# Moving the forward D2 reshuffles and the lower filter halves to ScalarE's DMA queue, with table maskings as broadcast VectorE products

## Chip, cores, metric

One core of one Trainium2 chip. The time is device microseconds (us) of one execution. A lower time is better. The profile is of one execution of each kernel.

## What is computed

The kernel computes the forward pass and all gradients of a block with two parts. The first part is a spectral filter on the layer-normalised input (2048 x 448). The second is an MLP over the 2048 tokens.

```python
def _A_ref(x, w_r, w_i):                       # spectral filter
    X = rfft2(x.astype(float32), axes=(-2, -1))
    return irfft2(X * (w_r + 1j * w_i), s=(S, D)).astype(bfloat16)
def _B_ref(x, w1, b1, w2, b2):                 # MLP over tokens, F = 1792
    u = gelu(einsum("bsd,sf->bdf", layernorm(x), w1) + b1)
    return transpose(einsum("bdf,fs->bds", u, w2) + b2)
h  = x + _A_ref(layernorm(x), A_w_r, A_w_i)
h2 = h + _B_ref(layernorm(h), B_w1, B_b1, B_w2, B_b2)
# outputs: h2 and the gradients for x, w_r, w_i, w1, b1, w2, b2 from grad_out
```

Only the forward transform of the filter, some 20 to 70 us into the kernel, is touched here. It has two stages. In the first, TensorE makes rows of the half-transformed input. ScalarE and VectorE evacuate them (copy them out) from PSUM, where TensorE writes its results, into staging tiles, and eight DMAs (the reshuffles, u = 0 to 7) scatter the staging tiles over the partitions of `D2`. The second stage multiplies with tables `Ut` and `Vt` and needs all of `D2`. Between these matmuls TensorE does others of the MLP's backward part (`ps_mm` in the profile), whose transposed blocks of `B_w2` are loaded by DMAs, the transpositions.

## The kernel before, where it is touched

SyncE issues every DMA here, in program order. `nc.sync` is SyncE, `nc.scalar` and `sc` are ScalarE, `ve` is VectorE, `gp_` is GpSimd.

```python
# the tables: eight masked products of 256 elements each, on whichever engine has room
for j in range(4):
    m = msk[:, j:j + 1]
    dj = d1[:, :, :, j - 1] if j else dst[:, :, 112:128]
    for o, c in ((d0[:, :, :, j], 0), (dj, 1)):
        if load[1] + 0.24 < load[0] + 0.38:
            ve.tensor_scalar(out=o, in0=cv[:, :, :, c], scalar1=m, scalar2=None, op0=ALU.mult)
        else:
            sc.activation(out=o, in_=cv[:, :, :, c], func=ACT.Copy, scale=m)
        yield
...
def w_load():      # spectral filter: four DMAs for the real part, then four for the imaginary part
    for c_, d in ((0, A_w_r), (1, A_w_i)):
        for p0, p1, j0, j1, row, dims in (...):
            nc.sync.dma_start(out=W_rows[p0:p1, c_, j0:j1, :], in_=bass.AP(...))
            yield
...
def row_b(h, quarters=False):
    ...            # one row: matmuls, then the evacuation into cs
    if c:
        defer(RESH_LAG, lambda: nc.sync.dma_start(out=D2[u:u + 121:8]..., in_=cs...), cs)   # reshuffle u
...
def load_w2T():    # one transposed block of B_w2 into a ring of five buffers
    nc.sync.dma_start_transpose(out=wT, in_=B_w2[j * P:(j + 1) * P, :]...)
...
def fwd_x(c2):     # begins the second stage
    if c2 == 0:
        for kind in "TWWWWTTT":        # T: a held transposition; W: an imaginary filter load
            if kind == "W":
                next(w_loads)
            elif held_w2:
                held_w2.pop(0)()
```

Program order on SyncE is therefore: reshuffles with real filter loads and transpositions between them, then reshuffle 7, then one held transposition, four imaginary filter loads, and more held transpositions. Nothing written in the program says that the later ones must follow reshuffle 7. They follow it only because SyncE waits for that reshuffle's evacuation. (In the profile, `ps_ff` and `ps_mm` are PSUM tiles, L218 and L82 are the helpers through which matmuls and the work of ScalarE and VectorE pass, and `rS`, `r`, `rX`, `UTt` are what an evacuation writes; `r<-r` is a reshuffle.)

## Time and profile before

| | before |
|---|---|
| time, median of 3 (range) | 359.86 us (359.79 to 361.12) |
| span, granted clock of the profiled run | 358.5 us, 0.989 |
| TensorE busy | 341.3 us, 95% |
| TensorE waits in 20 to 70 us | A 1.6 (ScalarE evacuation), B 1.4 (transposed block of B_w2), C 1.0 (ScalarE evacuation), 0.5 (VectorE) |
| last reshuffle: issued, landed | 46.66, 49.8 us |
| first matmul of the second stage | 50.34 us |

The lines of the profile stand in the prediction. "Landed" here and below is the time of the last semaphore count of a DMA in the trace. The granted clock is the share of full speed that TensorE was allowed.

### The profile page before, as it was taken

The numbers are of one execution on the slowest core, as the hardware profiler recorded it, in microseconds if no ns is written. First come the engines' busy times: TensorE is split into PE (matmuls) and PEld (weight loads), VectorE is DVE, ScalarE is ACT, GpSimd is POOL, SyncE is SP. The second block draws the span as 40 slices with busy tenths as digits, with TensorE's granted clock in tenths as the row PEclk, the third lists the DMA queues.
The fourth block names the chain that finished last, engine by engine and source line by source line (L and its number), as shares of the span: only waits on it lengthen the run. The fifth ranks groups of instructions, "written<-read, shape, count | busy, mean of one in ns | idle before, by whom it ended". The sixth has DMA issues, their size and how long they took to land.

```text
span 358.5 us, 6455 instructions
## 1 busy us (share of the span) xinstructions
PE 341.3 (95%) x2133; PEld 183.5 (51%) x2133; DVE 252.4 (70%) x676; ACT 214.9 (60%) x460; POOL 64.0 (18%) x227
## 2 busy tenths in 40 slices
PE   5888998899999999999999999999999999999994
PEld 2455665555645555555555555544445444455551
DVE  5896626991884888685327888784497766489895
ACT  4659836965986555503221455565478776478883
POOL 8667000000220000001001111110000000045462
PEclk9699999999999999999999999999999999999999
DMA  8999989747999999997976999969975878999995
GB/s 207 292 208 241 192 184 160 167 140 267 279 289 352 301 349 228 236 248 211 218 180 131 194 205 205 214 178 266 282 198 187 239 204 227 252 183 230 249 305 212
DMA packets 147673, 81.63 MB, mean 228 GB/s; under 512 B 95480, under 2 KB 139768, under 8 KB 147384
## 3 DMA queue, kind: packets, MB, share of 16 engines
q1 hardware_dynamic: 147640, 81.23, 94.1%
q8 instruction: 16, 0.26, 0.3%
q14 instruction: 17, 0.14, 0.1%
HBM read 27.56 MB, written 23.89 MB: 144 GB/s over the span
## 4 chain that ended last, share of the span: by engine, by line
PE 76%; DVE 8%; ACT 7%; DMA 4%; issue 3%; SPq 1%; POOL 0%; ACTq 0%; DVEq 0%
PE ps_mm L218 63%; PE ps_ff L218 13%; DVE r L82 4%; DMA rO<-in_B_w_dram 2%; ACT rO L82 2%; DVE stats L82 2%; DMA rA<-in_A_x_dram 1%; ACT rG L82 1%; ACT Ut L82 1%; DVE rA L82 1%; DVE rS L82 1%; SPq L297 1%; ACT r L82 1%; ACT Vt L82 1%; ACT rX L82 0%
## 5 line engine op out<-in xcount | busy, mean ns | idle before, releaser
L218 PEld LDWEIGHTS <-r 128*128 128x128 bf16 (+2 forms) x660 | 61.7, 104 | 50.8 <-issue 3.8
L218 PEld LDWEIGHTS <-rS 128*128 128x128 bf16 (+2 forms) x496 | 40.3, 98 | 39.3 <-issue 7.6
L218 PE MATMUL ps_mm<-rD,r 128*128 128x448 bf16 x224 | 44.5, 352 | 0.0
L82 ACT CAST rO<-ps_mm 128x512 bf16<-128x512 f32 (+1 forms) x63 | 33.7, 576 | 12.5 <-PE ps_mm L218 12.1
L218 PE MATMUL ps_mm<-rC,rE 128*128 128x448 bf16 x144 | 36.1, 370 | 3.2 <-DMA rC<-in_grad_out_dram 3.2
L218 PEld LDWEIGHTS <-rst 128*128 128x128 bf16 (+1 forms) x320 | 23.9, 97 | 29.3 <-issue 13.8
L82 ACT CAST r<-ps_ff 128x452 bf16<-128x452 f32 x58 | 33.5, 577 | 8.6 <-PE ps_ff L218 8.2
L218 PE MATMUL ps_mm<-r,rst 128*128 128x512 bf16 (+3 forms) x192 | 36.6, 353 | 0.0
L218 PE MATMUL ps_mm<-rB,r 128*128 128x448 bf16 x160 | 31.2, 352 | 0.1
L218 PE MATMUL ps_mm<-rG,rst 128*128 128x512 bf16 (+1 forms) x128 | 28.2, 380 | 0.0
L82 ACT ACTIVATE r<-ps_mm,rstd_h 128x448 bf16<-128x448 f32 x16 | 10.2, 635 | 26.0 <-PE ps_mm L218 26.0
L82 ACT ACTIVATE r<-rC 128x448 bf16<-128x448 bf16 x16 | 9.1, 572 | 26.8 <-DMA out_dram<-r 13.2
L82 DVE SCALAR_TENSOR_TENSOR r<-ps_mm,b2col,r 128x448 bf16<-128x448 f32 x16 | 10.9, 683 | 19.9 <-PE ps_mm L218 18.2
L82 DVE CAST rO<-ps_mm 128x512 bf16<-128x512 f32 x17 | 11.6, 689 | 16.3 <-PE ps_mm L218 15.4
L82 ACT ACTIVATE rG<-rG 128x896 bf16<-128x896 bf16 x14 | 13.3, 952 | 14.9 <-DVE rG L82 14.7
L218 PEld LDWEIGHTS <-rO 128*128 128x128 bf16 (+1 forms) x165 | 15.6, 98 | 12.1 <-DMA rO<-in_B_w_dram 1.7
L218 PE MATMUL ps_mm<-rE,rS 128*128 128x448 bf16 x112 | 21.5, 352 | 0.0
L82 ACT CAST rG<-ps_mm 128x512 bf16<-128x512 f32 (+1 forms) x35 | 17.2, 540 | 6.9 <-PE ps_mm L218 6.7
L218 PE MATMUL ps_mm<-rC,rO 128*128 128x448 bf16 x80 | 19.1, 352 | 1.4 <-DMA rO<-in_B_w_dram 1.4
L1180 POOL TENSOR_SCALAR lcol<-lcol 128x1 f32<-128x1 f32 x16 | 8.5, 532 | 65.1 <-ACT r L82 65.1
L218 PEld LDWEIGHTS <-rE 128*128 128x128 bf16 x148 | 14.3, 100 | 11.2 <-issue 4.9
L218 PE MATMUL ps_ff<-csI,rAT 113*128 113x224 bf16 (+1 forms) x108 | 19.0, 298 | 0.4 <-ACT rAT L82 0.2
(198 smaller groups left out, 645.4 us busy)
## 6 DMA issues: line engine op xcount, KB each, us to landing
out_dram<-rO SPq DMA_DIRECT2D x34, 256.0 KB
r<-in_B_w_dram SPq DMA_DIRECT2D x5, 1024.0 KB
r<-r SPq DMA_DIRECT2D x16, 226.0 KB
r<-r SPq DMA_DIRECT2D x32, 113.0 KB
rS<-in_B_w_dram SPq DMA_DIRECT2D x4, 896.0 KB
out_dram<-rG SPq DMA_DIRECT2D x10, 256.0 KB
rO<-in_B_w_dram SPq DMA_DIRECT2D x2, 1024.0 KB
out_dram<-rG SPq DMA_DIRECT2D x10, 192.0 KB
```

The costliest lines, as they stand in the source:

```text
L82: fn(**kw)
L218: nc.tensor.matmul(out, lhsT=lhsT, rhs=rhs, start=start, stop=stop)
L297: nc.sync.dma_start_transpose(out=wT, in_=B_w2[j * P:(j + 1) * P, :].rearrange("f (t c) -> f t c", c=P))
L1180: gp_.tensor_scalar(out=m1, in0=ms, scalar1=-1.0 / D, scalar2=None, op0=ALU.mult)
```

## The change

Intent: take ScalarE's small maskings away, give the freed time to DMA issue, and free SyncE so that held transpositions and filter loads go out earlier. The diff, cut to its core:

```diff
+    mskb = mem.tile([P, 1, 1, 4], BF16, name="mskb")
+    gp_.tensor_copy(out=mskb[:, 0, 0, :], in_=msk)
-            for j in range(4):
-                ...                       # eight products of 256 elements, VectorE or ScalarE
+            for out, c, j in ((d0, 0, 0), (d1, 1, 1)):
+                n = 4 - j
+                nc.vector.tensor_tensor(out=out, in0=cv[:, :, :, c:c + 1].broadcast_to([P, 16, 16, n]),
+                                        in1=mskb[:, 0:1, 0:1, j:4].broadcast_to([P, 16, 16, n]), op=ALU.mult)
+                yield True
+            evac_mask(dst[:, :, 112:128], cv[:, :, :, 1], msk[:, 0:1])
...
-                nc.sync.dma_start(out=W_rows[p0:p1, c_, j0:j1, :],
+                resh_eng(p0 == 0).dma_start(out=W_rows[p0:p1, c_, j0:j1, :],
...
-    def resh_eng():
-        _ei[0] += 1
-        return nc.sync
+    def resh_eng(on_act=True):
+        if not on_act:
+            return nc.sync
+        load[0] += 0.55
+        return nc.scalar
...
-            defer(RESH_LAG, lambda: nc.sync.dma_start(out=D2[u:u + 121:8]...
+            defer(RESH_LAG, lambda: resh_eng(not quarters).dma_start(out=D2[u:u + 121:8]...
```

`load` is the program's own estimate of each engine's work, by which it hands out evacuations while it is built. Each DMA issued on ScalarE adds 0.55 us to it, so the change can also move evacuations from ScalarE to VectorE.

More of the change, by code (lines that the diff above doesn't have):

```diff
@@ L463, with evac_mask @@
     comp_ring = ring(rO, 0, 2, 512)
+    mskb = mem.tile([P, 1, 1, 4], BF16, name="mskb")
+    def evac_mask(out, in_, m):
+        if load[1] + 0.43 < load[0] + 0.7:
+            ve.tensor_scalar(out=out, in0=in_, scalar1=m, scalar2=None, op0=ALU.mult)
+        else:
+            load[0] += 0.3
+            sc.activation(out=out, in_=in_, func=ACT.Copy, scale=m)
     def gen_UV():
@@ L502, in gen_UV @@
             d1 = dst[:, :, 64:112].rearrange("p g (l f) -> p g l f", f=3)
-            for j in range(4):
-                m = msk[:, j:j + 1]
-                dj = d1[:, :, :, j - 1] if j else dst[:, :, 112:128]
-                for o, c in ((d0[:, :, :, j], 0), (dj, 1)):
-                    if load[1] + 0.24 < load[0] + 0.38:
-                        ve.tensor_scalar(out=o, in0=cv[:, :, :, c], scalar1=m, scalar2=None, op0=ALU.mult)
-                    else:
-                        sc.activation(out=o, in_=cv[:, :, :, c], func=ACT.Copy, scale=m)
-                    yield
+            for out, c, j in ((d0, 0, 0), (d1, 1, 1)):
+                n = 4 - j
+                load[1] += 0.06 + 256.0 * n / 960.0
+                nc.vector.tensor_tensor(out=out, in0=cv[:, :, :, c:c + 1].broadcast_to([P, 16, 16, n]),
+                                        in1=mskb[:, 0:1, 0:1, j:4].broadcast_to([P, 16, 16, n]), op=ALU.mult)
+                yield True
+            evac_mask(dst[:, :, 112:128], cv[:, :, :, 1], msk[:, 0:1])
+            yield
     Rp = rO[:, 1536:1536 + P]
@@ L692, in row_b @@
         if c:
-            defer(RESH_LAG, lambda: nc.sync.dma_start(out=D2[u:u + 121:8].rearrange("p g c k -> p (g c k)"),
+            defer(RESH_LAG, lambda: resh_eng(not quarters).dma_start(out=D2[u:u + 121:8].rearrange("p g c k -> p (g c k)"),
                                                       in_=cs.rearrange("p x c k -> p (x c k)")), cs)
```

## The prediction

> **What bounds the kernel now.** I read the page's busy shares first, then the table of stretches, then the waits of TensorE, then the chain that ended last between 20 and 70 us, and last the timelines of the single engines and of the SyncE queue. The busy shares:
>
> ```profile
> PE 341.3 (95%) x2133; PEld 183.5 (51%) x2133; DVE 252.4 (70%) x676; ACT 214.9 (60%) x460; POOL 64.0 (18%) x227
> ```
>
> TensorE is the bound: 358.5 - 341.3 = 17.2 us of the span are all that it is not busy, and a change that leaves its work alone can win only from these. The change touches the forward transform, which by the tiles' use lies between 20 and 70 us:
>
> ```profile
> 20.00:30.00 10.00, 7.90 (x59) 4.77 (x57) 9.96 (x37) 7.40 (x15) 7.66 (x30) 1.00 1.00 208
> 30.00:40.00 10.00, 9.94 (x84) 7.04 (x85) 6.43 (x23) 8.67 (x18) 4.57 (x21) 1.00 1.13 244
> 40.00:50.00 10.00, 9.95 (x73) 6.24 (x71) 4.55 (x11) 5.20 (x11) 0.11 (x1) 1.00 0.79 144
> 50.00:60.00 10.00, 9.13 (x72) 5.87 (x70) 5.99 (x18) 6.97 (x18) 0.11 (x1) 1.00 1.18 191
> 60.00:70.00 10.00, 8.48 (x54) 5.27 (x55) 7.96 (x18) 8.28 (x13) 0.00 (x0) 1.00 0.95 197
> ```
>
> The columns are the stretch, its length, then busy time of PE, PEld, DVE, ACT, POOL, the clock, the DMA share and GB/s. TensorE is idle 10 - 7.90 = 2.1, then 0.06, 0.05, 0.87 and 1.52 us: 4.6 us together, 1.3% of the span. That is the ceiling of the whole change. The waits of TensorE in this window name nearly all of it:
>
> ```profile
> PE ps_ff L218 <- ACT rS L82: 1.6, 1, 1.6
> PE ps_mm L218 <- DMA rO<-in_B_w_dram: 1.4, 1, 1.4
> PE ps_ff L218 <- ACT rX L82: 1.0, 1, 1.0
> PE ps_ff L218 <- DVE rX L82: 0.5, 1, 0.5
> ```
>
> Call the first wait A, the second B, the third C. The chain shows what stands ahead of A: two and three table maskings on ScalarE round one row's evacuations, and only then the evacuation that TensorE waits for at 30.07 us.
>
> ```profile
> 25.79 1.08 ACT Ut L82 x2
> 26.87 0.47 ACT rS L82
> 27.34 0.44 ACT r L82
> 27.77 1.81 ACT Ut L82 x3
> 29.59 0.43 ACT rS L82
> ```
>
> B is a late transposed block of B_w2. SyncE's timeline shows why it is late:
>
> ```profile
> 46.66 0.53 SPq L693 DMA_DIRECT2D r<-r  x1
> 47.28 2.26 SPq L297 DMA_TRANSPOSE rO<-in_B_w_dram  x1
> 49.59 2.35 SPq L583 DMA_DIRECT2D rB<-in_A_w_i_dram  x4
> 52.05 4.87 SPq L297 DMA_TRANSPOSE rO<-in_B_w_dram  x1
> ```
>
> SyncE issues in program order. The last reshuffle of D2 (L693) waits until 46.66 us for its evacuation; the held transposes and the imaginary filter loads (L583) stand behind it. The transpose of 52.05 us is the one that TensorE waits for; the chain gives it 8.48 us to 60.5.
>
> C belongs to another part: from 62.1 to 68.0 us ScalarE copies five filter quarters of 0.95 us each between evacuations. The change doesn't take those copies away.
>
> **What the Trainium skill says.** "VectorE: DVE Perf Modes", What auto-detection actually checks: two elements per cycle need every tensor to be 16-bit with step 1 or -1. The trace agrees for packed operands: the 128x904 bf16 products took 625 ns, the 128x448 ones 384 to 392, so 456 more elements cost about 237 ns, 1.9 per ns at 0.96 GHz. The new products read one operand with an innermost step of zero, so I take one element per cycle; no row of this trace has that form.
>
> "ScalarE: Activation LUTs", What ACT_TABLE_LOAD costs: 186 ns + 0.833 N, some 93 ns more per pointer operand, back-to-back overlap 93 ns. For 256 elements with a pointer scale that is about 0.40 us from one to the next. The trace differs: two maskings took 1.08 us and three 1.81 in the chain, 0.54 to 0.60 each. I use the trace.
>
> "DMA: Bandwidth & Descriptors", Queues, rings and completion order and Issuing engines are not separate DMA queues: SP and ACT each own one ring per DMA engine, each ring is consumed in order, the rings are served in turn, and a second issuer saves sequencer time but no bandwidth. The trace agrees on the order within a ring: the reshuffle issued at 36.62 us, behind a filter load, has its last semaphore count at 44.6, 8.0 us later, while that of 46.66, with little ahead of it, is complete at 49.8, 3.1 us later.
>
> **The change part by part.**
>
> 1. Table maskings. Removed: 16 products of 256 elements. On ScalarE ran 6 of Ut and 5 of Vt, at 0.55 us each 11 x 0.55 = 6.0 us; on VectorE 2 and 3, at about 0.33 us back to back (three in 0.99) 5 x 0.33 = 1.7 us. Added: per table one product of 1024 and one of 768 elements on VectorE, at 0.96 per ns plus 0.06 us back to back (0.625 - 904/1920 = 0.15 of fixed time, less 0.09 that neighbours overlap): 1.13 + 0.86 = 2.0 us, so 4.0 us for both; and one remaining masking per table, 0.33 or 0.55 us on either engine. GpSimd gets one four-element copy. ScalarE loses about 5 to 6 us, VectorE gains 2.3 to 3.0.
>  On the path: A. Of the Ut maskings five stand in ScalarE's row between 25.79 and 29.59 us, about 2.8 us, and the sixth follows. Without them the evacuation at 29.59 can come as soon as its matmuls end, near 28 us. VectorE is full until 30 us (9.96 of 10), and the Ut products put 2.0 - 0.7 = 1.3 us more there. It is not late then, though: its row scalings were 0.5 us ahead of the matmuls that read them near 23.8 us and 1.7 us ahead near 27.5, and after 33.3 us VectorE idles 2.6 us. I count A down from 1.6 to about 0.4 us: -1.2 us.
>
> 2. D2 reshuffles. Eight issues of 0.53 to 0.68 us leave SyncE for ScalarE's sequencer: 8 x 0.55 = 4.4 us, two of them before 31 us, six between 33 and 47. Two filter loads of 450 KB follow, 1.2 us. So ScalarE gives back almost all that part 1 freed, 5.6 against 5 to 6 us, but spread over 25 us in which it has room (8.67 of 10 between 30 and 40, 5.20 between 40 and 50). An evacuation there is needed only a row later, some 1.75 us, so one issue of 0.55 us in front of it costs TensorE little. I count +0.2.
>
> 3. Freed SyncE. Its next transpose then waits only for its ring slot, whose matmuls end near 34 us, not for the reshuffle at 46.66. I expect it at about 36 us instead of 47.3, the upper imaginary loads near 38 to 40, and the transpose that B waits for near 40 us, when its own slot is read out (38.9 us). It is then down long before 59 us, and B vanishes: -1.4 us. ScalarE and VectorE sat idle waiting for matmuls through most of B (1.55 and 1.84 us), so I expect their work behind it to shift along, and C to stay at about 1.0.
>
> 4. What the earlier transfers collide with. By the packets in the trace, a transpose is 2048 packets of 256 bytes of some 19 ns, /16 engines = 2.4 us; the upper imaginary loads also about 2.4. Between 35 and 48 us the queue now carries about 11 us of work in 13 us; two transposes and these loads add 7.2, so the engines are full until about 49. The last reshuffle competes with them. The second-stage matmul at 50.3 us needs all eight reshuffles; the last one's data landed at 49.8, so only 0.5 us is spare, and if A is gone that matmul is due at 49.1. ScalarE's own ring gives the reshuffle a share in turn, 128 packets of 1808 bytes, so I expect a wait of 0 to 1.5 us: +0.7.
>
> Sum: -1.2 + 0.2 - 1.4 + 0.7 = -1.7 us, and 359.86 - 1.7 = 358.2. After 105 us TensorE is 10.00 of 10 in every stretch to 150, so a shift earned before it is carried through. A few tenths more may come from the earlier start of later D3 reshuffles and of the filter placing on SyncE: I predict 357.9 us.
>
> **The rivals.** (i) The reshuffles land late. If ring turns favour the long filter packets (some 550 ns against 140), the last reshuffle could be 3 to 5 us late, and the second stage starts late: 360 to 363 us. For it speaks the DMA share above 1.1 around it; against it, that few such packets are left by 46 us and that the loads' lower halves are in the same ring as the reshuffles, behind them. (ii) VectorE becomes the bound of the first rows: it is full from 10 to 30 us, and if the broadcast products cost 1.5 us instead of 1.13, the row scalings come late and A is replaced by a wait of like size: 359 to 360. Against it speaks its idle time after 33 us. (iii) Everything works: A, B and the 0.5 us wait go, and the evacuations are shared out so that C shrinks too: 4.6 us at most minus small rests, 355.5 to 356.5. (iv) B's gain is taken by ScalarE, which is 8.28 of 10 from 60 to 70 us; then C grows by some 1 us: about 359.
>
> **Range and chances.** The middle, between (i) and (iii), is 357.9; eight times in ten 355.9 to 360.8. Over 2% faster would be under 352.7, 7.2 us of gain against a ceiling of 4.6: 0.02. Over 2% slower, above 367.1, needs seven late us at the second stage: 0.03. Within 2%: 0.95.
>
> **What would show it.** Right: no TensorE wait on the ScalarE rS evacuation above 0.6 us between 25 and 31; no wait on a transposed block near 59; SyncE's first held transpose before 40 us; broadcast products of 1.2 and 0.95 us as the trace counts them; second-stage matmuls starting within 1 us of 50. Wrong: a wait of the second stage on D2 over 2 us, row matmuls waiting for VectorE's rX or rS over 1 us in all after 23 us, or C above 2 us.

## The result, and the profile after

| | before, same rounds | after |
|---|---|---|
| median (range), 4 runs each | 359.83 us (359.02 to 361.12) | 369.56 us (368.17 to 369.9) |
| ratio, 95% interval | | 1.026 [1.0219, 1.030] |
| span and clock of the profiled run | 358.5 us, 0.989 | 368.1 us, 0.970 |
| first matmul of the second stage | 50.34 us | 61.86 us |

The changed kernel is 2.6% slower. A ratio here is the mean time of one kernel's fast runs over that of the other's of the same rounds, so it is not quite the ratio of the medians.

**Where the time went.** The stretches of the kernel after, with the columns as in the prediction (PE, PEld, DVE, ACT, POOL, clock, DMA share, GB/s):

```profile
30.00:40.00 10.00, 6.53 (x53) 4.20 (x52) 7.18 (x22) 3.88 (x8) 7.15 (x22) 0.94 1.14 227
40.00:50.00 10.00, 7.97 (x38) 4.75 (x37) 1.55 (x3) 3.54 (x8) 0.00 (x0) 0.50 1.07 197
50.00:60.00 10.00, 10.00 (x65) 6.25 (x63) 3.81 (x8) 2.83 (x5) 0.11 (x1) 0.87 1.10 183
```

Compare 30 to 40 us: before, PE was 9.94 busy and ACT 8.67. Now they are 6.53 and 3.88. Both idle. From 40 to 50 us PE looks fairly busy, but the clock column says 0.50: half speed, and 38 matmul instructions are counted where there had been 73. TensorE's waits from 18 to 75 us:

```profile
PE ps_ff L218 <- ACT rS L82: 3.5, 1, 3.5
PE ps_ff L218 <- ACT r L82: 2.0, 1, 2.0
PE ps_ff L218 <- DMA r<-r: 1.6, 1, 1.6
```

(The list goes on with 1.0 us for a transposed block at 28.56 us.) The first two name ScalarE evacuations; the third is the second stage waiting for the last reshuffle. Wait A at 28 to 30 us is gone, but the 1.0 us for the transposed block stand in its place. B at 59 us is gone, and C fell from 1.0 to 0.7. Most of what the prediction wanted to win was won, and more was lost.

**Why ScalarE was late.** Its timeline; the bracket is the idle time before a line and what ended it:

```profile
38.04 0.63 ACTq L592 DMA_DIRECT2D rB<-in_A_w_r_dram  x1
38.71 0.53 ACT L82 CAST rD<-ps_mm 128x448 bf16<-128x448 f32 x1 [5.27 <-DMA rE<-in_B_w_dram]
...
45.40 0.57 ACTq L704 DMA_DIRECT2D r<-r  x1
46.01 0.54 ACT L82 CAST r<-ps_ff 128x452 bf16<-128x452 f32 x1 [5.35 <-DMA rB<-in_A_w_r_dram]
...
56.33 0.54 ACTq L704 DMA_DIRECT2D r<-r  x1
```

Read the second line. An evacuation that reads only PSUM is said to have waited 5.27 us for a transposition of B_w2, with which it shares no data. What waited was the DMA issue in the line above, and the evacuation stood behind it, because ScalarE runs in order. The DMA records in the trace, which carry the number of each DMA's completion semaphore (the counter by which it reports its end), show why the issue waited. The DMAs of SyncE and ScalarE use eight such semaphores in turn, one set for both engines. The instruction records name the waits: the first issue waits for semaphore 107, the second for 101, and each came when the previous user of that semaphore had landed:

| DMA on ScalarE | its semaphore's previous user | previous user landed | issued |
|---|---|---|---|
| real filter load, lower half (L592) | transposition issued on SyncE at 32.26 | 38.02 | 38.04 |
| reshuffle 4 (L704) | real filter load issued on SyncE at 38.57 | 45.30 | 45.40 |

Before, no such wait occurs here: between 20 and 70 us SyncE's waits are for TensorE and for evacuations, and the semaphore of reshuffle 4, which went out at 36.62 us, had been free since 30.98. A rival reading, that ScalarE cannot issue while SyncE issues a transposition, fails in the same trace: reshuffle 5 went out on ScalarE at 48.83 us, inside SyncE's issue of a transposition from 46.80 to 52.96. The Trainium skill, "DMA: Bandwidth & Descriptors", Anatomy of one DMA, says that DMA engines do not wait on semaphores and that such a wait is made on the issuing sequencer. The trace agrees: 5.27 and 5.35 us of ScalarE's idle time.

**Why the clock fell.** TensorE stood idle for 3.5 us up to 39.79 us. The clock record of the trace has half speed from 38.89 to 52.54 us, and in this time the same matmuls took 1.32 us in place of 0.73. Three matmuls of 128x448 before, then after:

```profile
19.84 0.73 PE L218 MATMUL ps_mm<-rC,rE 128*128 128x448 bf16 x3
```

```profile
46.98 1.32 PE L218 MATMUL ps_mm<-rC,rE 128*128 128x448 bf16 x3
```

The Trainium skill, "TensorE: Matmul & The Clock Gate", What's actually happening, says that an idle window of about 3.4 us halves the clock and that about 3.4 us of sustained work restores it. The trace differs in the first: half speed began 2.6 us after TensorE's last matmul had ended at 36.32 us. The same section calls the window free-running, that is, not started by the kernel, and with that the return agrees: half speed lasted 13.65 us, four times the section's 3.41 us. In the first three of these four stretches TensorE still had idle time (the rest of the 3.47 us, then the 2.03 us up to 46.60). The fourth was full, and at its end the clock came back.

**The sum.** The second stage started 61.86 - 50.34 = 11.5 us later. TensorE's idle waits up to there are 0.54 + 1.05 + 3.47 + 2.03 + 1.55 = 8.6 us after, and 0.36 + 0.54 + 1.62 = 2.5 us before: 6.1 us more. At half clock, TensorE was busy some 0.2 + 8.0 + 2.6 = 10.8 us (the 2.6 from the mean clock 0.87 of 50 to 60 us), and half of that, 5.4 us, is lost speed. 6.1 + 5.4 = 11.5, an estimate that fits. B (1.4 us) and 0.3 us of C are then won back, and the span ends 9.6 us later.

**What SyncE did with its freedom.** Its queue after:

```profile
39.69 5.11 SPq L297 DMA_TRANSPOSE rO<-in_B_w_dram  x1
44.84 1.86 SPq L592 DMA_DIRECT2D rB<-in_A_w_i_dram  x3
46.80 6.16 SPq L297 DMA_TRANSPOSE rO<-in_B_w_dram  x1
```

Before, these three came at 47.28, 49.59 and 52.05 us, behind reshuffle 7. Now the first precedes reshuffles 4 to 7 (issued 45.40, 48.83, 54.28, 56.33 us) and all three precede 5 to 7. Before, the block of the first was first read at 53.07 us and that of the last at 60.57: work that is needed later goes ahead of work that is needed at 50. Reshuffle 7 was issued 9.7 us later than before and took 5.4 us instead of 3.1.

One more thing is slow, early on: a transposition issued on SyncE at 19.41 us and reshuffle 0, issued on ScalarE at 19.52, landed at 28.52 and 26.43 us. Before, the transposition of 19.66 landed at 24.4. By the packets in the trace, the DMA engines moved 121 GB/s from 22 to 28 us in the kernel after (112 to 129 in stretches of 2 us), against 197 before.

### The profile page after: what moved, and what is told of

The parts are those of the page before. It is cut to its first block, busy times and chain, and to the rows that moved or that the text cites. A ratio compares the mean times of both kernels' runs of the same rounds, so it can differ in the third digit from the quotient of the medians.

```text
span 368.1 us, 6441 instructions
## 1 busy us (share of the span) xinstructions
PE 346.2 (94%) x2133; PEld 185.4 (50%) x2133; DVE 255.4 (69%) x675; ACT 210.7 (57%) x451; POOL 68.3 (19%) x228
## 4 chain that ended last, share of the span: by engine, by line
PE 76%; DMA 7%; DVE 6%; ACT 6%; issue 2%; SPq 2%; POOL 0%; ACTq 0%; DVEq 0%
PE ps_mm L218 62%; PE ps_ff L218 14%; DVE r L82 3%; DMA rO<-in_B_w_dram 2%; ACT rO L82 2%; DMA rB<-in_A_w_r_dram 2%; DMA r<-r 1%; ACT rG L82 1%; SPq L297 1%; DMA rA<-in_A_x_dram 1%; DVE stats L82 1%; ACT rX L82 1%; DVE rA L82 1%; ACT r L82 1%; ACT rAT L82 0%
## 5 line engine op out<-in xcount | busy, mean ns | idle before, releaser
L218 PEld LDWEIGHTS <-rS 128*128 128x128 bf16 (+2 forms) x496 | 41.3, 100 | 42.5 <-issue 9.6
L218 PE MATMUL ps_mm<-rC,rE 128*128 128x448 bf16 x144 | 38.3, 386 | 2.9 <-DMA rC<-in_grad_out_dram 2.4
L82 ACT CAST rG<-ps_mm 128x512 bf16<-128x512 f32 (+1 forms) x35 | 17.2, 540 | 6.9 <-PE ps_mm L218 6.7
L218 PE MATMUL ps_mm<-rC,rO 128*128 128x448 bf16 x80 | 19.9, 367 | 1.0 <-DMA rO<-in_B_w_dram 1.0
L82 ACT CAST rS<-ps_ff 128x512 bf16<-128x512 f32 x30 | 17.5, 583 | 3.6 <-PE ps_ff L218 3.6
```

Of the source, the lines that this page charges most:

```text
L82: fn(**kw)
L218: nc.tensor.matmul(out, lhsT=lhsT, rhs=rhs, start=start, stop=stop)
```

## The experiments

Four explanations are named in the expectations. **L**: an issue on ScalarE waits for the semaphore of an earlier DMA, and ScalarE's evacuations wait behind it. **V**: the broadcast products on VectorE cost more than they save. **Q**: the DMA issues take ScalarE's own time. **M**: SyncE, no longer held by the reshuffles, sends transpositions and imaginary filter loads ahead of them, so the reshuffles land late. (A rival B in one expectation, two rings that slow each other, is close to M; it is not wait B.)

### The parts one by one

`a1_masks` is the kernel before with only the mask change; `a2_reshuffles` with only the reshuffles on ScalarE; `a3_filter` with only the lower filter halves (the loads whose part starts at `p0 == 0`) on ScalarE; `a4_queues` with both moves and the old masks.

```diff
# a2_reshuffles, against before
-            defer(RESH_LAG, lambda: nc.sync.dma_start(out=D2[...
+            defer(RESH_LAG, lambda: resh_eng(not quarters).dma_start(out=D2[...
# a3_filter, against before
-                nc.sync.dma_start(out=W_rows[...
+                resh_eng(p0 == 0).dma_start(out=W_rows[...
# a1_masks: the change without these two lines; a4_queues: these two lines without the masks
```

> The kernel before with the broadcast mask products alone; every DMA stays on SyncE. Theory L (ScalarE, which runs in order, is held up at its DMA issues by the completion semaphore of an earlier DMA, because eight semaphores are shared by both queues): no issue on ScalarE, so no such wait; TensorE's wait A of 1.6 us shrinks and the time is 357.5 to 359.5, no slower than before (359.8). Rival V (the broadcast products on VectorE hold up the rows): 363 or more, with TensorE waits on VectorE of several us between 20 and 45 us.

> The kernel before with the eight D2 reshuffles alone on ScalarE. Theory L: each waits on ScalarE until the DMA that last had its semaphore is down; where that is a transpose issued shortly before, ScalarE idles for 2 to 5 us. The filter load on ScalarE, which had the first long wait after the change, is not there, so the cost should be smaller than the whole: 361 to 366. Rival Q (the 0.55 us that each issue costs ScalarE): 8 x 0.55 = 4.4 us spread, most of it hidden, 360 to 361, no ScalarE idle time that ends with a DMA. Rival B (two rings at once slow each other): reshuffles land 5 to 7 us after their issue instead of 3, the second stage starts late without any long ScalarE idle time.

> The kernel before with the lower halves of the filter alone on ScalarE. Theory L: one load in the rows and one at the second stage, each waiting for its semaphore's last user; in the built program the one in the rows has the semaphore that a transpose or a load had eight DMAs earlier. If that one is down by then, 359 to 361; if not, ScalarE idles up to 5 us and TensorE drops its clock, up to 366. Rival Q: 359.5 to 360.5, since two issues are 1.2 us.

> The whole change without the mask products. Theory L: the loss is all here, 366 to 371, with ScalarE idle for over 3 us at two DMA issues and the granted clock at half speed for some us after. Rival V: about 360, the loss stays with the products.

| | median (range), us | ratio to before, 95% |
|---|---|---|
| before, same rounds | 359.1 (357.2 to 360.31) | |
| a1_masks | 359.24 (358.83 to 359.6) | 1.0003 [0.9965, 1.004] |
| a2_reshuffles | 369.19 (368.06 to 371.61) | 1.0289 [1.0234, 1.0343] |
| a3_filter | 359.38 (358.31 to 360.03) | 1.0004 [0.9964, 1.0044] |
| a4_queues | two fast runs 365.54, 363.84; two slow, 371.44 and 371.97 | not given |

The reshuffles alone make the whole loss, more than the 361 to 366 us expected; masks and filter halves alone show no change. V falls. `a4_queues` spreads too widely for a ratio; its fast runs lie below the 366 to 371 expected. TensorE's waits in `a2_reshuffles`:

```profile
PE ps_ff L218 <- ACT UTt L82: 5.2, 1, 5.2
PE ps_ff L218 <- DMA r<-r: 4.8, 1, 4.8
```

Here reshuffle 4 waited on ScalarE for its semaphore, whose previous user, a transposition issued at 31.88, landed at 42.20, and went out at 42.61 us. ScalarE was idle for 6.2 us round it. So the same two effects appear with no filter load on ScalarE: an evacuation stuck behind an issue, and a last reshuffle that lands late (53.34 to 61.56 us).

The mask change did what it should at A: `a1_masks` has PE 9.46 busy of 10 from 20 to 30 us, against 7.90 before. At B it lost a little:

```profile
PE ps_mm L218 <- DMA rO<-in_B_w_dram: 1.7, 1, 1.7
```

B was 1.4 us before: TensorE arrives at the late transposed block earlier and waits 0.3 us longer for it. The rest of the gain is still in this trace behind all these waits: the first matmul that reads `RTm` starts at 85.49 us, against 86.80 before. The times don't show it. Their interval reaches from 1.3 us of gain to 1.4 us of loss, so a gain of this size is neither shown nor excluded.

### SyncE held again, and other issuers

`c1_gate` is the kernel after, with SyncE made to wait: a tiny copy on SyncE that reads the last staged row, placed behind the last reshuffle.

```diff
+    gate = mem.tile([16, 2], BF16, name="gate")
...
+            if u == NT // 2 - 1 and not quarters:
+                defer(RESH_LAG, lambda: nc.sync.dma_start(out=gate[:], in_=cs[0:16, 1, 1, 0:2]))
```

`c2_pool` is the kernel before with reshuffles 3 to 7 issued by GpSimd; `c3_act` the same by ScalarE. Neither has the mask change.

```diff
-            defer(RESH_LAG, lambda: nc.sync.dma_start(out=D2[...
+            defer(RESH_LAG, lambda: (gp_ if u >= 3 and not quarters else nc.sync).dma_start(out=D2[...   # c2_pool
+            defer(RESH_LAG, lambda: (nc.scalar if u >= 3 and not quarters else nc.sync).dma_start(out=D2[...   # c3_act
```

`c4_warm` is the kernel after with 18 idle matmuls in each of rows 11 and 12, so that TensorE is not idle long enough to lose its clock.

```diff
+    def warm_pe(n):
+        idle_ = ps_mm()
+        for _ in range(n):
+            nc.tensor.matmul(idle_[:, 0:D], lhsT=Rm[:], rhs=go_tp[:, 0, :], start=True, stop=True)
...
+        if t == 11:
+            warm_pe(18)
         row_b(t - 1)
+        if t == 12:
+            warm_pe(18)
```

> The changed kernel whole, with one tiny copy of four bytes on 16 partitions on SyncE behind the last reshuffle, which reads the rows staged for it: SyncE is held there again, so that its held transposes and imaginary loads go out no earlier than in the kernel before, and the semaphores of the ScalarE issues are now those of DMAs that came down earlier. Theory L plus M (the freed SyncE sends transposes and loads ahead, they fill the semaphore ring and mix with the reshuffles of the other ring): nearly the whole loss goes, 358 to 362, no ScalarE idle time over 2 us that a DMA ends. Rival Q (that ScalarE issues DMAs at all, whatever SyncE does): it stays at 366 to 370.

> The kernel before with the reshuffles 3 to 7 on GpSimd's queue, the first three on SyncE as before. GpSimd's DMAs have no completion semaphores in common with SyncE's, and ScalarE issues nothing; SyncE is freed as in the change and runs ahead. Theory L alone: nothing blocks ScalarE, so 357 to 361. Theory M alone (mixing makes the reshuffles land late): the second stage still waits 3 us or more for the last reshuffle, 363 to 368. With both, in between: 360 to 364.

> The twin of the GpSimd run: the same reshuffles 3 to 7, but on ScalarE. In the built program its second waits for the semaphore of the transpose issued last before the filter loads. Theory L: ScalarE idle for 4 us or more at one of the issues, 364 to 370. If it is as fast as the GpSimd run, L is not the cause.

> The changed kernel whole with 2 x 18 idle matmuls of 448 columns on TensorE, placed where it waits in rows 11 and 12 (their result is never read). Each block is 18 x 0.19 = 3.4 us, about as long as the waits of 3.5 and 2.0 us that it fills. Theory C (the granted clock falls to half after such a wait and costs time of its own): the clock stays at 1.0 between 38 and 53 us and the time falls by 1.5 to 4 us against the changed kernel's 369.6, to 365.5 to 368. If the clock costs nothing because TensorE only waits for ScalarE there, it stays at 369 to 371.

| | median (range), us | ratio to before, 95% |
|---|---|---|
| before, same rounds | 359.89 (359.44 to 360.62) | |
| c1_gate | fast 359.78, 359.39; slow 365.74, 365.22 | 0.9993 [0.9973, 1.0013] (fast runs) |
| c2_pool | 368.97 (365.19 to 369.55) | 1.0228 [1.0166, 1.029] |
| c3_act | 369.56 (369.04 to 371.01) | 1.0277 [1.0253, 1.03] |
| c4_warm | 366.98 (364.34 to 368.85) | 1.0193 [1.0144, 1.0242] |

**c1_gate.** In its fast runs all of the loss is gone, while every reshuffle and lower filter half is still issued by ScalarE, with the mask products on VectorE. So in these runs the issues as such cost nothing that counts, and Q falls with V. The gate does two things at once: it holds the later transfers back, and, since the held transposition no longer takes a semaphore early, the lower filter load on ScalarE gets another one. That one had been free since 29.36 us, and the load went out at 33.02 us instead of 38.04. `c2_pool` separates the two. SyncE's queue of `c1_gate`, where the gate is followed by the held transposition at almost its old time (47.28 before):

```profile
45.37 0.59 SPq L708 DMA_DIRECT2D gate<-r  x1
46.06 2.40 SPq L297 DMA_TRANSPOSE rO<-in_B_w_dram  x1
```

Two of its four runs were at 365 us and were told slow. On one core this label rests on their time alone (over 1.5% above the fastest run), so it may also be the loss that came back in part: with all four runs the median is 362.5 us. I don't explain them from this run; `e1_gate_late` below looks at them.

**c2_pool.** No reshuffle of 3 to 7 is on ScalarE, and ScalarE has no wait on a DMA in the window. The loss is nearly as large all the same, in one piece (its interval reaches below 1.02, so that it is slower is clear, that it is over 2% slower is not; the same holds for `c4_warm`). The wait of TensorE, then the issues of SyncE and GpSimd (GpSimd's carries the label POOL):

```profile
PE ps_ff L218 <- DMA r<-r: 8.9, 1, 8.9
```

```profile
37.67 7.29 SPq L297 DMA_TRANSPOSE rO<-in_B_w_dram  x1
...
45.01 3.04 SPq L583 DMA_DIRECT2D rB<-in_A_w_i_dram  x4
46.54 0.53 POOL L693 DMA_DIRECT2D r<-r  x1 [1.05 <-DVE r L82]
```

The last reshuffle was issued at 46.54 us, as early as before (46.66). It landed at 58.29, 11.75 us later, where it took 3.1 before. In front of it SyncE had put a transposition (37.67, landed 51.9) and three filter loads (from 45.01, landed 54 to 58.1); the fourth followed at 46.92. GpSimd's queue is not slow in itself: its reshuffle of 33.85 us, before all these, landed after 4.54 us, and one on SyncE at 34.44 after 4.64. So a block on ScalarE isn't needed for the loss. The median lies 1 us above the 363 to 368 expected of M and far above the 357 to 361 of L alone. `c3_act` shows a mixture: 7.1 us for the reshuffle, 2.2 for a ScalarE evacuation, and the same total, with two idle times of 2.6 us on ScalarE where 4 or more were expected. It has no added `load`, so the handing out of evacuations isn't the cause either. This speaks for M as what suffices; the wait of L comes on top where ScalarE issues, and both begin with SyncE running ahead.

**c4_warm.** With idle matmuls the clock stays up here:

```profile
40.00:50.00 10.00, 10.00 (x79) 6.42 (x77) 3.47 (x8) 2.91 (x7) 0.00 (x0) 1.00 1.12 174
```

The time falls from a ratio of 1.026 to 1.0193, about 0.007 x 360 = 2.5 us (the two ratios are of different rounds, and their intervals touch, so the size is rough). That is less than the 5.4 us of lost speed in the sum above: the second stage waits for the late reshuffles instead (2.2 us on `r<-r` in this run, and PE 7.36 of 10 from 50 to 60 us). After that wait the clock fell once more, to 0.50 from 59.7 to 63.1 us, so this run doesn't measure the clock's full worth. Most of the loss stays with a full clock up to 59 us: the halved clock is a consequence that adds to the loss, not its first cause.

### The gate again, wait B after the mask change, and the transfers by themselves

`e1_gate_late` is `c1_gate` with reshuffles 0 to 2 left on SyncE. `d1_order` is `a1_masks` with the second held transposition ahead of the imaginary filter loads. `d2_cap` is `a1_masks` with a transposition released earlier. `e2_micro` is a separate kernel with wrong outputs: phases of transpositions and reshuffle copies with nothing beside them, each phase run twice and closed by VectorE.

```diff
# e1_gate_late, against c1_gate
-            defer(RESH_LAG, lambda: resh_eng(not quarters).dma_start(...
+            defer(RESH_LAG, lambda: resh_eng(u >= 3 and not quarters).dma_start(...
# d1_order, against a1_masks
-            for kind in "TWWWWTTT":
+            for kind in "TTWWWWTT":
# d2_cap, against a1_masks
-CAP = 8
+CAP = 9
# e2_micro: the body of one repetition; T(j) is a transposition of 128 rows of B_w2 on SyncE, C(j, eng) a reshuffle copy
+        for j in range(4): T(j)                              # alone
+        for j in range(4): C(j, act)                         # alone
+        for j in range(4): T(j); C(j, sp)                    # one ring
+        for j in range(4): C(j, act); T(j)                   # two rings
+        for j in range(4): C(j, sp if j % 2 else act)        # control
```

> The gate of c1_gate (a tiny copy on SyncE that reads the last row's evacuation, so that SyncE waits for the last reshuffle again), but reshuffles 0 to 2 are left on SyncE and only 3 to 7 go out on ScalarE. Theory (order of the late transfers decides; the slow runs of c1_gate at 365 us came from the early transposition and the first reshuffle, 0.1 us apart on two rings): 358 to 360.5 us in every run, none at 365. If the slow runs of c1_gate have another cause, some of these are at 364 to 366 us too. If ScalarE's issues or the VectorE products were the loss, 364 us or more in all.

> The mask change alone, with the order of what SyncE still holds at the last reshuffle turned: the second transposition ahead of the imaginary filter loads, not behind them. Theory (what the masks gained at the first wait was given back at the wait for the late transposed block of B_w2): that wait shrinks from 1.7 us to under 0.5 and the time is 357 to 358.5 us. If the gain of the masks is lost elsewhere, 359 to 360 us as with the masks alone.

> The mask change alone, with the row group's cap raised from 8 to 9 so that a held transposition may be released one step earlier. Same theory as d1_order by another way: 357.5 to 359 us if the late block is the cost; 359 to 360 if not. Weaker than d1_order, because the cap also moves other work.

> A kernel of its own with wrong outputs on purpose: eight or four DMAs at a time with nothing beside them, each phase run twice and closed by a wait of VectorE: four transpositions alone on SyncE's ring, four reshuffle copies alone on ScalarE's ring, both kinds in turn on SyncE's ring, copies on ScalarE's with transpositions on SyncE's ring, and as a control two and two of each kind on both rings. Estimates from the traces (2.4 to 2.9 us for a transposition, 1.6 us for a copy at full rate): 11.6, 6.5 and some 16 to 18 us for the first three. If a transposition beside copies of another ring is slow in itself, the two-ring phase takes 20 us or more; if the slowness seen from 19 to 28 us had another cause, 16 us or less.

| | median (range), us | ratio to before, 95% |
|---|---|---|
| before, same rounds | 359.16 (357.4 to 360.02) | |
| e1_gate_late | 360.5 (360.13 to 362.38) | 1.0056 [1.0025, 1.0087] |
| d1_order | 357.87 (357.23 to 358.62) | 0.9972 [0.9941, 1.0003] |
| d2_cap | 360.03 (358.55 to 361.23) | 1.003 [0.9994, 1.0065] |

**e1_gate_late.** Six runs, all fast, none near 365 us. Three of them (360.55, 361.08, 362.38) are above the expected 360.5, so the range was a little too low. The result again says that holding SyncE removes most of the loss: 1.0056 against 1.026. Here the gate went out at 47.04 us, and the held transposition behind it at 47.72. The interval excludes 1, so some 2 us remain, to which ScalarE's issues (Q) may contribute. Six runs without a slow one, against two slow in four, fit the idea that the early start of two rings (a ring is one engine's queue on the DMA engines) made `c1_gate`'s slow runs, but they don't prove it. That stays open.

**d1_order.** B is gone, as expected, and the median is inside the expected range. TensorE's largest waits:

```profile
PE ps_ff L218 <- ACT rX L82: 1.2, 1, 1.2
PE ps_ff L218 <- DVE rS L82: 0.9, 1, 0.9
```

The transposition now goes out at 49.46 us (51.40 in `a1_masks`) and lands at 53.94. This has the lowest median, with the masks, everything on SyncE, and two letters exchanged. Its interval still includes 1.000, by a hair, so "1 us faster than before" is not shown. Nor is a gain from the new order: the first matmul that reads `RTm` starts at 85.47 us here and at 85.49 in `a1_masks`, so in these two traces the waits above took what B had cost, and the ratios (0.9972 and 1.0003, of different rounds) have overlapping intervals.

**d2_cap** missed: a transposition released at 36.00 us, ahead of reshuffles 4 to 7 in the same ring, took B out of the waits and put a 1.7 us wait on the last reshuffle (`r<-r`) in its place. The last reshuffle landed at 50.84 us. The wait is that of theory M in small, on one queue; the time (interval 0.9994 to 1.0065) is not shown to differ from before.

**e2_micro.** This is one execution. Phase times between VectorE's closings, second repetition: transpositions alone 69.6 to 81.0, 11.4 us; copies alone 82.1 to 88.4, 6.3; both in turn on one ring 88.6 to 103.6, 15.0; on two rings 103.7 to 120.9, 17.2 (16.4 in the first repetition). The control, as built, has four copies on two rings and no transposition (the expectation says "of each kind"); it took 6.3, as on one ring. My expectation was 20 us or more if two rings are slow in themselves and at most 16 if not; the answer lies between, so two rings cost 1.4 to 2.2 us of throughput, 9 to 15%. They don't explain the 112 to 129 GB/s of 22 to 28 us in the kernel after. What grows more is the time of the single transfer. DMA issues, with KB each and median us from issue to landing; first copies alone, then one ring, then two rings:

```profile
D<-cs ACTq DMA_DIRECT2D x4, 226.0 KB, 3.9
...
D<-cs SPq DMA_DIRECT2D x4, 226.0 KB, 3.2
wt<-in_B_w_dram SPq DMA_TRANSPOSE x4, 4.6
...
D<-cs ACTq DMA_DIRECT2D x4, 226.0 KB, 6.3
wt<-in_B_w_dram SPq DMA_TRANSPOSE x4, 7.3
```

On two rings the last of the four copies, issued at 47.70 and 105.94 us, took 10.1 and 10.5 us; alone, the last of four took 4.3. A separate ring gives a copy no right of way over transpositions that are under way. In the kernel, where reshuffle 7 is what the second stage waits for, this fits the 5.4 us of the kernel after and, with filter loads in addition, the 11.75 us of `c2_pool`; it was not isolated there.

## Why the prediction was wrong

The time was 369.56 us against 357.9 predicted and a range up to 360.8. By its own steps:

1. **Table maskings: right.** The products took 1.224 us for 1024 elements and 0.925 to 0.950 for 768, as "1.2 and 0.95 us" had it. The wait on ScalarE's evacuation at A is gone. VectorE didn't become the bound: its rX wait stayed at 0.5 us.

```profile
L516 DVE TENSOR_TENSOR Ut<-rO,mskb 128x1024 bf16<-128x1024 bf16 x1 | 1.2, 1224 | 0.0
...
L516 DVE TENSOR_TENSOR Ut<-rO,mskb 128x768 bf16<-128x768 bf16 x1 | 0.9, 925 | 0.0
```

   What A is worth alone stays open: the trace of `a1_masks` keeps a lead of 1.3 us at 85 us, its times show none (ratio 1.0003, 0.9965 to 1.004).

2. **Reshuffles on ScalarE, "+0.2": wrong, about +5.5 us of waits.** The step counted issue time (8 x 0.55 us) and nothing else. It took the wait of an issue to be its evacuation, as on SyncE. It did not see that an issue also waits for the previous user of its semaphore, the DMA eight before it in the program's order, that this set of semaphores is common to both engines, and that ScalarE carries this wait into its evacuations: 5.27 and 5.35 us idle, which TensorE felt as 3.47 and 2.03 us. And it did not see that the clock would halve with such a wait.

3. **Freed SyncE, "-1.4": right in what it wins, wrong in calling it free.** The held transposition went out at 39.7 us (36 predicted, "before 40" in the list of signs), and B vanished. But that early issue is where the loss begins. `c1_gate` and `e1_gate_late` take it away and keep ScalarE's issues (the second those of reshuffles 3 to 7): 0.9993 in the fast runs of the first, 1.0056 in all six of the second.

4. **Collision, "+0.7": the mis-sized term.** The step had the right transfers (two transpositions and the filter loads against the last reshuffle) and read a separate ring as a fair share that leaves a wait of 0 to 1.5 us. In the kernel after, the direct wait was 1.55 us, under the sign of "over 2 us", but only because TensorE itself came some 10 us late; the second stage began at 61.86 us where the list of signs asked for "within 1 us of 50". In `c2_pool`, where ScalarE was not blocked and TensorE came in time, the wait was 8.9 us. The spare 0.5 us at 50.3 us had been noted, and it was the warning: nothing that delays the last reshuffle is hidden.

Of the rivals, (i) named the mechanism, late reshuffles, and put it at 360 to 363 us. It was dismissed because "few such packets are left by 46 us" and because the lower halves would be behind the reshuffles. The imaginary loads were put near 38 to 40 us, but three went out from 44.84 to 46.7; and the lower real half went out at 38.04, ahead of reshuffles 4 to 7. `e2_micro` shows besides that transpositions alone, without filter packets, delay the copies. (ii) fell with the masks' measured times. (iii) and (iv) did not arise.

The chance of 0.03 for slower came from "seven late us at the second stage" seeming far away. It was 11.5.

Shown: the reshuffles' move alone makes the loss, holding SyncE removes most of it, and a blocked ScalarE is not needed for it. Read from the trace, not isolated: that the shared semaphores were what held ScalarE. Open: how the loss in the kernel after divides between the late landing and the blocked ScalarE, why the first transfers (19 to 28 us) are so slow there, and the slow runs of `c1_gate`.

## What to carry to other kernels

A DMA that waits on its queue may be ordering everything behind it; before moving it elsewhere, list what will then overtake it and when each overtaker is needed. Move a DMA to a computing engine only after asking what its issue can wait for, because the engine's own work waits with it. When a wait is taken away, look for the next one on the same path: in `d1_order` two letters in the order of held transfers took B away, and other waits stood in its place.

## What the Trainium skill lacked or had wrong

- "DMA: Bandwidth & Descriptors": it places semaphore waits on the issuing sequencer, but does not say that a program may give both HWDGE engines one set of eight completion semaphores in turn, so that an issue on ScalarE can wait for SyncE's DMA eight before it. Here: 5.27 and 5.35 us of ScalarE's time.
- "DMA: Bandwidth & Descriptors", Rules for kernel authors: a transpose next to ordinary DMAs is said to need nothing. That is about correctness and agrees with the correct results here. That all DMAs share the engines and interleave is said under Issuing engines are not separate DMA queues; how long a copy then takes is not: copies beside transpositions of another ring landed after 6.3 us (median) instead of 3.9 alone, the last after 10.1 to 10.5 instead of 4.3.
- "TensorE: Matmul & The Clock Gate", What's actually happening: an idle window of about 3.4 us is said to halve the clock. Here less was enough: in the kernel after, half speed began 2.6 us after the last matmul, and in `c4_warm` it followed a wait of 2.17 us.
